# Eight products of the unit matrix between two rows of a weight product, and a later start of one unit's attention pieces

## The chip, the cores and the metric

The kernel runs on one core of a Trainium2 chip. The metric is the device time of one launch in microseconds. The core has five engines that run side by side, each through its own instructions in order: TensorE (PE in the profile; its weight loads, which overlap its matmuls, are PEld), VectorE (DVE), ScalarE (ACT), GpSimd (POOL), and SyncE (SP), which here only issues DMAs. TensorE's clock can be granted at full or at reduced speed, which the profile shows as PEclk.

## The reference

```python
def _attn_ref(q, k, v, a_re, a_im):                    # 4 batches, 8 heads, 768 steps, 48 channels
    mag = np.sqrt(a_re * a_re + a_im * a_im)
    scale = np.minimum(mag, 0.999) / (mag + 1e-06)
    a_re_n, a_im_n = (a_re * scale, a_im * scale)
    for t in range(S):
        ar, ai = (a_re_n[:, :, t, :, None], a_im_n[:, :, t, :, None])
        new_re = ar * S_re - ai * S_im
        new_im = ar * S_im + ai * S_re
        kv = np.einsum('bhd,bhe->bhde', k[:, :, t], v[:, :, t])
        S_re, S_im = (new_re + kv, new_im)
        y[:, :, t] = np.einsum('bhd,bhde->bhe', q[:, :, t], S_re)
...
def _moe_ref(x, w1, w2, w3, w_out):                    # 3072 tokens of 384, inner width 1024
    a = x @ w1
    b = x @ w2
    h = a * b @ w3
    return (h @ w_out).astype(np.float32)
```

The four weight matrices arrive as 64-bit floats; the rest is 32-bit.

## The kernel before, in words

**Units.** The work is cut into eight units: four batches, and two halves of 384 steps in each. A unit goes through three stages.

1. Gates (`gates`): elementwise work on ACT and DVE over tiles of 128 x 1152 that turns the gates, q and k into scaled and rotated forms. `gates` is a generator whose steps are named, among them `im` and `sq` (L600, L604 on DVE), `z1` (a Ln on ACT, the first use of L586 after `sq`), `n` (L614), `z2` and `a2`. It also issues loads for the next unit: the `im` part of the next gates is loaded when two products, `kc` and `qc` (L717, L719), are through, since its buffer comes free then. When a unit's gates are done, twelve DMAs move the results into tiles KL and QL (L736).
2. Pieces (`pieces`): for each of three chunks of 128 steps, two transposes on PE (`tr`, L766), each followed by a copy into tile KT on ACT (L768); a state product (`kv`, L830), followed by an addition into T on DVE (L836); scores (`sc`, L780) into two PSUM banks, followed by two masked copies into A on DVE (L783); and outputs (`y`, L813), followed by a copy into xT on ACT (L815).
3. Feed-forward (`ffn`): sixteen halves. Each is three 128-deep products of a 128-column block of w1 or w2 with xT (L852), giving m; an even half is copied to `a` by ACT (L857) and an odd one multiplied with it by DVE into `ab` (L859). After them come sums (`sum`, four So operations on DVE, L887) and seven products p (L912: p1, p2, p4, p6, p7, p5, p3) by which two token tiles are multiplied with the folded weight w3o; p1, p2 and p4 do not read So.

**Buffers.** The transposes, kv and y share two PSUM buffers in turn (`ps_v`), so that every such tile waits until the one two before it has been read: the third transpose waits for the first copy into KT. The halves and products share four (`ps_m`).

**The start.** The product of w3 and w_out (w3o) is made first, on chip, in eight rows of 128: `row_load` fetches a row of both weights, `row_work` rounds it from 64 to 32 bits on DVE and ACT (L997 to L1014; w3s and wo_s are the results, w3s in two buffers in turn, so that row f+2 is written only when PE is done with row f), and `fuse` adds, for each of eight column blocks j, one 128 x 128 by 128 x 384 product into one of eight PSUM sums (L1150). After row 7 ACT copies the sums to w3o (L1154). In the same stretch DVE and ACT work through unit 0's gates, and SP issues the loads of unit 1's gates and of the weights w1 and w2, the moves of unit 0 into KL and QL, and then fourteen loads of v into tile V (L560), which `y` needs.

**Order.** Up to row 7, a scheduler orders DVE, ACT, POOL and SP by its own model of times, PE's order is the program's. From there the order on all engines is written out by `run`, which walks a list of PE's items and puts each step of the gates (and of the weights' rounding) where a planner with a table of durations expects its inputs to be ready. `unit(u, rest, ahead)` makes the list for unit u: the first `ahead` halves of unit u-1's feed-forward, and then unit u's pieces with what is left of that feed-forward spread between them. `ahead` is AHEAD[u].

## Time and profile before

| | us |
|---|---|
| median of three runs | 552.43 (551.7 to 552.54) |
| the profiled execution, its whole time | 552.92 |
| its span | 551.1 |
| PE busy | 521.0 (95% of the span) |
| DVE busy | 372.6 |
| POOL busy | 358.0 |
| ACT busy | 275.3 |

The whole time of the profiled execution is its span and 1.8 us around it. A row of the timeline reads: start, length, engine, line, operation, output <- inputs, shape, how often; in brackets how long the engine had been idle before, and who ended that. A matmul of 32-bit operands leaves two records, a transpose one, so that a row of fuse (8 products) is 16 records and a half (3 products) is 6. A view of windows gives for each stretch its length, PE's busy time with the number of records that began in it, the mean granted clock, and the DMA engines' busy share and rate.

### The profile page before, as it was taken

What the parts mean: (1) busy time and instruction counts of PE and PEld (TensorE: products, weight loads), DVE (VectorE), ACT (ScalarE), POOL (GpSimd) and SP (SyncE); (2) the same over time, 40 slices, a digit from 0 to 9 for tenths busy, and PEclk for the clock granted to TensorE, in tenths of its full rate; (3) what the DMA queues carried; (4) which work ended last, traced back from release to release, by engine and by line L of the source; (5) the groups of instructions that cost most, each with busy time, mean ns of one, the idle gap of its engine ahead of it and who ended that gap; (6) DMA issues with size and microseconds to landing.
All of it is one profiled execution on the core that took longest, in us unless ns stands there. A gap on an engine that the chain in (4) does not pass through costs nothing.

```text
span 551.1 us, 13443 instructions
## 1 busy us (share of the span) xinstructions
PE 521.0 (95%) x5546; PEld 370.0 (67%) x5546; DVE 372.6 (68%) x553; ACT 275.3 (50%) x391; POOL 358.0 (65%) x425
## 2 busy tenths in 40 slices
PE   4689899989999999989999999999999999999995
PEld 2345575556756795669568985687569966795585
DVE  5999589775585677867977985687669751531152
ACT  5989766465543555746467426743494232111100
POOL 1000000188888788888998888988998888888100
PEclk9899899999999999989999999999999999999999
DMA  8997956966659835492889346935793173222001
GB/s 262 339 395 236 212 167 189 253 161 162 159 141 242 223 106 132 146 207 84 245 212 218 112 129 165 215 110 152 170 224 100 58 205 83 73 65 96 1 26 39
DMA packets 73510, 89.73 MB, mean 163 GB/s; under 512 B 31840, under 2 KB 63264, under 8 KB 72672
## 3 DMA queue, kind: packets, MB, share of 16 engines
q1 hardware_dynamic: 67360, 69.78, 48.2%
q0 software_dynamic: 6080, 19.01, 11.7%
q8 instruction: 45, 0.74, 0.6%
q14 instruction: 25, 0.20, 0.1%
HBM read 65.14 MB, written 4.72 MB: 127 GB/s over the span
## 4 chain that ended last, share of the span: by engine, by line
PE 67%; DVE 14%; DMA 8%; ACT 5%; issue 3%; SPq 1%; DVEq 0%; ACTq 0%
PE m L852 35%; PE p L912 14%; PE y L813 6%; PE sc L780 5%; PE o L948 3%; DMA im<-in_a_im_dram 2%; DMA QL<-q 2%; DMA raw<-in_w_dram 2%; DVE gZ L687 2%; PE kv L830 2%; PE tp L766 2%; ACT low L1002 1%; DVE So L887 1%; DMA out_dram<-ot 1%; ACT gZ L586 1%
## 5 line engine op out<-in xcount | busy, mean ns | idle before, releaser
L852 PE MATMUL m<-xT,w1s 128*128 128x384 f32 x384 | 134.5, 487 | 1.1 <-ACT xT L815 1.1
L852 PE MATMUL m<-xT,w2s 128*128 128x384 f32 x384 | 134.8, 487 | 0.0
L852 PEld LDWEIGHTS m<-xT,w1s 128*128 128x128 f32 x384 | 72.2, 190 | 48.9 <-ACT xT L815 1.7
L852 PEld LDWEIGHTS m<-xT,w2s 128*128 128x128 f32 x384 | 71.9, 190 | 47.8
L1069 POOL TENSOR_SCALAR look<-look 128x256 f32<-128x256 f32 (+1 forms) x84 | 86.7, 1032 | 7.3
L1050 POOL TENSOR_TENSOR seen<-seen,look 128x256 bf16<-128x256 bf16 (+1 forms) x84 | 80.9, 963 | 6.8
L859 DVE TENSOR_TENSOR ab<-m,a 128x384 f32<-128x384 f32 x64 | 35.2, 551 | 69.8 <-PE m L852 66.3
L857 ACT COPY a<-m 128x384 f32<-128x384 f32 x64 | 30.2, 473 | 95.1 <-PE m L852 95.1
L1034 POOL MEMSET seen<- 128x256 bf16 x1 | 0.3, 311 | 102.3 <-DVE w2s L1014 102.3
L1068 POOL TENSOR_SCALAR look<-look 128x256 f32<-128x256 f32 (+1 forms) x44 | 51.7, 1174 | 6.1 <-DMA look<-in_a_re_dram 2.8
L1066 POOL TENSOR_TENSOR look<-look 128x256 f32<-128x256 f32 (+1 forms) x72 | 48.6, 675 | 3.5 <-DMA look<-in_w_dram 1.7
L912 PE MATMUL p<-To,So 128*128 128x192 f32 x240 | 44.1, 332 | 0.0
L1045 POOL DMA_DIRECT2D look<-in_w_dram x56 | 33.1, 591 | 16.6 <-POOL seen L1050 16.6
L815 ACT COPY xT<-y 128x384 f32<-128x384 f32 x24 | 11.5, 478 | 60.2 <-PE y L813 60.2
L1071 POOL TENSOR_TENSOR look<-look 128x256 f32<-128x256 f32 (+1 forms) x44 | 38.1, 866 | 3.7
L912 PEld LDWEIGHTS p<-To,So 128*128 128x128 f32 x240 | 38.7, 190 | 2.2 <-issue 2.0
L768 ACT COPY KT<-tp 128x384 f32<-128x384 f32 x40 | 34.0, 857 | 11.9 <-PE tp L766 11.7
L813 PE MATMUL y<-A,V 128*32 128x128 f32 x768 | 39.8, 273 | 0.1
L783 DVE COPY_PREDICATED A<-mask,sc 128x512 f32<-128x512 uint8 x48 | 32.7, 733 | 6.4 <-PE sc L780 6.2
L813 PE MATMUL y<-QL,T 96*32 96x128 f32 x640 | 35.5, 272 | 0.8 <-issue 0.8
L813 PEld LDWEIGHTS y<-A,V 128*32 128x32 f32 x768 | 34.3, 110 | 2.1 <-issue 2.0
L1150 PE MATMUL f<-wo_s,w3s 128*128 128x384 f32 x96 | 35.6, 520 | 0.0
(129 smaller groups left out, 922.4 us busy)
## 6 DMA issues: line engine op xcount, KB each, us to landing
look<-in_w_dram POOLq DMA_DIRECT2D x56, 256.0 KB, 4.0
raw<-in_w_dram SPq DMA_DIRECT2D x6, 1024.0 KB, 10.7
KL<-gR SPq DMA_DIRECT2D x24, 192.5 KB, 4.6
KL<-k SPq DMA_DIRECT2D x24, 192.5 KB, 6.1
re<-in_a_re_dram SPq DMA_DIRECT2D x24, 192.0 KB, 4.4
im<-in_a_im_dram SPq DMA_DIRECT2D x24, 192.0 KB, 4.0
k<-in_k_dram SPq DMA_DIRECT2D x24, 192.0 KB, 8.1
q<-in_q_dram SPq DMA_DIRECT2D x24, 192.0 KB, 7.4
```

The source lines that it names most:

```text
L768: nc.scalar.copy(out=KT_t[u, c][:, :, :, x].rearrange("p h d f -> p f d h"), in_=tp.rearrange("p f (d h) -> p f d h", h=H))
L813: nc.tensor.matmul(out=o, lhsT=a, rhs=b, start=s0, stop=s1)
L852: nc.tensor.matmul(out=m, lhsT=w[:, j * P // WB, f, j * P % WB:j * P % WB + P], rhs=xT_t[u][:, f], start=(f == 0), stop=(f == KD - 1))
L859: nc.vector.tensor_tensor(out=ab_t[u][:, j], in0=m, in1=got[0], op=OP.mult)
L912: nc.tensor.matmul(out=m[p], lhsT=a[:, f], rhs=b[:, f], start=(f == 0), stop=(f == KH - 1))
L1045: nc.gpsimd.dma_start(out=got.bitcast(I32)[:, 0:group[2]], in_=group[1])
L1050: nc.gpsimd.tensor_tensor(out=seen[:, 0:n], in0=seen[:, 0:n], in1=x, op=OP.add)
L1066: tt(out=x, in0=x, in1=x, op=OP.mult)
L1068: ts(out=y, in0=x, scalar1=high, scalar2=None, op0=OP.is_le)
L1069: ts(out=x, in0=x, scalar1=low, scalar2=None, op0=OP.is_ge)
L1071: tt(out=x, in0=x, in1=y, op=OP.mult)
L1150: nc.tensor.matmul(out=sums[j], lhsT=w3_t[f][:, j * P:(j + 1) * P], rhs=w3_t["wo"][:, f], start=(f == 0), stop=(f == KF - 1))
```

## The change

```diff
-    AHEAD = [0, 3, 12, 12] + [8] * (NU - 4)
+    AHEAD = [0, 3, 12, 15] + [8] * (NU - 4)
...
-    sums = []
+    sums, spare = [], []
 
     def fuse(f, j):
         if not sums:
             sums.extend([sc.rearrange("p n t -> p (n t)")[:, 0:DM] for sc in Sc] +
                         [ps_v.tile([P, DM], FP, tag="v", name="f") for _ in range(2)] +
-                        [ps_m.tile([P, DM], FP, tag="mm", name="f") for _ in range(4)])
+                        [ps_m.tile([P, DM], FP, tag="mm", name="f") for _ in range(3)])
+            spare.append(ps_m.tile([P, SB * LANES * LANES], FP, tag="mm", name="f"))
+            sums.append(spare[0][:, 0:DM])
+        for _ in range(8 if (f, j) == (4, 0) else 0):
+            nc.tensor.matmul(out=spare[0][:, DM:DM + P], lhsT=ident, rhs=ident, start=False, stop=False)
         nc.tensor.matmul(out=sums[j], lhsT=w3_t[f][:, j * P:(j + 1) * P], rhs=w3_t["wo"][:, f], start=(f == 0),
                          stop=(f == KF - 1))
```

Ahead of row 4's first product PE multiplies the 128 x 128 unit matrix by itself eight times. The result goes to the last 128 columns of the eighth sum's PSUM bank, columns 384 to 511, which nothing reads. The eighth sum is now the first 384 columns of a tile that has the whole bank.

Unit 3's pieces begin when fifteen of the sixteen halves of unit 2's feed-forward are through, rather than twelve. Of unit 2's 25 feed-forward items ten rather than thirteen are left to stand between unit 3's pieces. PE's order from the thirteenth half on, before and after (tr, kv and sc with their chunk):

```
before: ab12 tr0 ab13 tr0' ab14 ab15 tr1 kv0 tr1' p1 kv1 p2 p4 sc0 p6 sc1 y0 p7 sc2 y1 y2 p5 p3
after:  ab12 ab13 ab14 ab15 tr0 tr0' p1 tr1 kv0 p2 tr1' p4 kv1 p6 sc0 p7 sc1 y0 sc2 y1 y2 p5 p3
```

The built programs differ on the other engines in three places. On DVE, all of row 7's rounding now stands ahead of the gate step `gA` (L744) that stood before its last operation, and two later steps of those gates, k and q, change places; on ACT row 7's last copy (L1002, 128 x 384) stands ahead of one gate step. In unit 3's stretch DVE does the four So before the first addition into T and swaps a few neighbours (T, gA, A, U), and ACT does `z1` before all four of the copies into KT, where it stood between the second and the third. SP and POOL issue the same DMAs and operations in the same order.

## The prediction

> **What bounds the kernel now.** I read the busy shares first (PE 95%), then the row of granted clocks, then PE's idle time in order, and last the chain of waits.

> ```profile
> PE 521.0 (95%) x5546; PEld 370.0 (67%) x5546; DVE 372.6 (68%) x553; ACT 275.3 (50%) x391; POOL 358.0 (65%) x425
> PEclk9899899999999999989999999999999999999999
> ```

> PE bounds the kernel, and three slices out of forty have a lower clock. PE's timeline around the first place that the change touches, and around the second:

> ```profile
> 35.54 2.42 PE L1150 MATMUL f<-wo_s,w3s 128*128 128x384 f32 x7
> 40.26 2.93 PE L1150 MATMUL sc<-wo_s,w3s 128*128 128x384 f32 x4 [2.30 <-DVE wo_s L1014]
> 42.98 4.34 PE L1150 MATMUL f<-wo_s,w3s 128*128 128x384 f32 x12
> 47.16 1.45 PE L1150 MATMUL sc<-wo_s,w3s 128*128 128x384 f32 x4
> ...
> 237.02 0.88 PE L830 MATMUL kv<-vr,KT 128*32 128x48 f32 x48
> 240.27 0.55 PE L766 MATMUL tp<-ident,k 128*128 128x128 f32 x3 [2.37 <-ACT KT L768]
> ```

> After each idle time the next matmuls are slow: row 4's sixteen records take 6.90 us (40.26 to 47.16), row 5's 5.16 (47.16 to 52.32). Two windows before and after each tell why:

> ```profile
> 36.72:40.13 3.41, 1.24 (x4) 1.00 1.02 413
> 40.13:43.54 3.41, 3.28 (x5) 0.51 1.00 387
> ...
> 118.63:122.04 3.41, 1.94 (x11) 1.00 1.07 241
> 238.16:241.57 3.41, 1.30 (x9) 1.00 1.11 231
> 241.57:244.98 3.41, 3.41 (x55) 0.50 1.10 248
> ```

> The chain of waits tells what a gain at the start would have to pass:

> ```profile
> 70.33 1.91 DMA V<-in_v_dram
> 72.25 1.32 PE sc L780 x57
> 75.84 1.37 DVE A L783 x2
> ...
> 114.78 3.61 DMA im<-in_a_im_dram
> 118.57 1.36 issue
> 119.92 0.56 DVE ab L859
> 120.52 0.91 PE o L948 x2
> ```

> **The products.** Eight products of two records each; a record of 384 columns takes 0.322 us at full clock (row 5: 5.16 over 16), so one of 128 columns about 0.107, and the eight 1.72 us. The nearest other row, a transpose (three in 0.33 us), gives 0.9. They run where PE waits 2.30 us for DVE's wo_s, which does not wait for them, so either length fits: the cost on the path is nothing, and should row 3 end 0.6 us later their excess would show one for one. At 1.72 us the idle time in the window falls to 0.5 to 0.6, below the 1.47 that kept the clock; at 0.9 to 1.4, just below it. Row 4 then runs in 5.16 us and ends 1.7 us earlier, at 45.4. DVE had waited for that row too:

> ```profile
> 47.36 0.69 DVE L1009 TENSOR_SCALAR w3s<-raw 128x1024 int32<-128x1024 int32 x1 [0.76 <-DMA re<-in_a_re_dram]
> ```

> The DMA named there had nothing to do with it; w3s has two buffers, and row 6's can only be written when row 4 is through (47.16). So DVE's row 6 begins 0.76 us earlier. With row 7's rounding moved ahead of a gate step (its 0.55 us) PE can go through rows 5, 6 and 7 without a stop, and begins row 7 at about 55.85 instead of 57.48: 1.6 us won there. ACT's copies out of the sums (it waited 2.62 us for the first), unit 0's transposes and kv, and unit 1's first gates hang on that and come 1.6 us earlier.

> What of it lasts? SP's queue does not move: the moves into KL and QL begin when the loads of w1 and w2 have landed (53.5), and the fourteen loads of V end with issues at 72.7 and 73.3 that land 3.5 and 3.0 us later, at 76.2 to 76.3. The first y starts at 76.14 and needs the last head some 0.65 us later, so PE itself can gain only 0.5 us there. DVE gains more. It did its masked copies of the third scores at 78.50, behind 1.15 us of waiting for PE and a heap of gate and rounding steps, all of which now lie before y; the third scores would be done at about 77.2. The buffer that SP's next load of weights waits for (issued 80.10), the V loads and weights behind it, and through them the DVE steps that end with ab at 119.92, follow that copy: 1.3 us. I take 1.3 us; the ends are 0 (the V loads keep it all) and 1.65 (all of it lasts). From 120 on PE is the chain almost everywhere, so what is won there stays.

> [...]

> **Unit 3.** Moved: four tr, two kv, three sc and three y on PE, with four copies into KT, two T, six A and three xT behind them; none of them issues a DMA, and the order on SP and POOL stays. PE's idle 2.37 us at 240.27 ends with a copy into KT, which stood in ACT's queue behind `z1` (238.23 to 239.48); `z1` waits for `sq` (until 238.12), that for `im` on DVE at 235.04, and that for the DMA im, issued at 229.28 when `qc` was done. None of these moves. What moves is what PE has to do meanwhile. Before: four halves, three tr, kv0, until 237.9. After: four halves from 228.20 (7.75 us), two tr (0.66) and p1 (1.30), until 237.9. Then tr1 waits for the first copy, which now is itself behind `z1`: 240.27 again. kv0 waits for the second copy, 0.84 us long, until 241.0: 0.35 us more idle. Behind `z1` on ACT now stand all four copies and p1's U; each waiter is on PE. The window to 241.57 has 0.9 us of work, so half clock follows as before, 1.7 us.

> From there the same set of items (to sc0 and p6) ends at 249.9 by the durations of the trace, against 249.96. DVE's four So (3.2 us) end at 241.8 with p6 at 247.3, so they stay hidden; if they were not, p6 would come up to 3.2 us later. Taken: -0.1 us. The ends: +0.9 (the wait for the second copy and one more U and copy in full) and -4.1 (idle 2.37 and 1.7 of clock both gone).

> **The sum.** -1.3 - 0.1 = -1.4 us. The profiled execution took 552.92 (span 551.1 and 1.8 around it): 551.5. It stands 0.5 above the median of 552.43, from which the same difference gives 551.0; I say 551.2, 0.2% below the median. About 0.2% (1.1 us) is what a measurement can tell from no change.

> **The rivals.**
> - *The V loads keep the gain*, or the products do not keep the clock. For: V lands 0.1 to 0.2 us after y starts. Against: DVE's backlog is what the chain names. -0.1 us: 552.3.
> - *The wait at 120.52 grows and costs the clock*: slower. PE arrives there earlier, but ab is last in a row of DVE steps behind the DMA im (114.78). If SP and DVE stay put and PE gains 0.5 us or more, the idle time of 1.47 passes 2.0, and the next window runs at half: +1.7, with 0.1 to 0.5 won elsewhere: 553.8. It decides once PE gains 0.1 to 0.6 us more than DVE. Against: the chain runs through PE's scores and DVE's copies, so DVE should gain at least as much.
> - *Unit 3's stop goes*: if im lands 0.9 us earlier, or the window's boundary splits the idle time, 1.7 to 4.1 us go as well: 549.5 down to 547.0. For: only 0.1 to 0.7 us separate the idle time in that window (2.11) from the limit. Against: the DMA's issue hangs on DVE's `qc`, which does not move.

> **How the numbers follow.** Forecast 0.48, V loads 0.21, growing wait 0.18, unit 3's stop 0.13. The range 549.0 to 553.9 holds the forecast, the V loads, the larger part of the growing wait, and the part of the last in which only the clock is won. The forecast's own range, from 1.65 won with a little luck in unit 3 to 0.8 won, is 550.2 to 551.7; about a quarter of it (above 551.3) lies within 0.2%. Faster 0.36 + 0.13 = 0.49; the same 0.12 + 0.17 = 0.29; slower 0.18 and, of the V loads' case, 0.04 with unit 3's upper end: 0.22.

> **What would show it.** Products: x16 at L1153 in the gap, row 4 in 5.2 us at clock 1.00, row 7 ready for ACT's first w3o copy near 56.7 instead of 58.33. V: a wait on V at the first y. DVE: the masked copy of 78.50 near 77.2, the load of 80.10 near 78.8, ab of 119.92 near 118.6, and an idle time there of 1.5 or less. Unit 3: an idle time near 2.3 us before its third transpose, ended by KT, another of 0.35, and half clock after. I am wrong if row 4 is still slow, if PE's wait near 120 exceeds 2 us, or if unit 3's stop is under 1.5.

## The result and the profile after

The changed kernel took 551.84 us in the median of 20 runs (546.78 to 555.88), the kernel before, run in turn with it, 552.55 (548.47 to 556.88): a ratio of 0.9976, with a 95% interval of 0.9953 to 1.0. Two later comparisons of the same pair, with 12 runs of the changed kernel each, gave 0.9993 (0.996 to 1.0025) and 0.9994 (0.9951 to 1.0036). The differences of the three means are -1.29, -0.73 and -0.49 us, with standard errors of 0.8 to 0.9; weighted together -0.9 +- 0.5. So by these means the change gains a little, 0.1 to 0.2%, close to what these runs can tell from nothing. A ratio leaves out the runs over 1.5% above the fastest of their kernel, a difference of means takes all, so that the two can disagree, most for ahead_only below, where the ratio rests on 7 of 12 runs.

The profiled execution took 548.02 (span 546.1). First the page's busy times and granted clocks, then PE's timeline at the places that the prediction spoke of (start, length, engine, line, operation, output <- inputs, count; in brackets the idle time before and who ended it):

```profile
PE 518.3 (95%) x5562; PEld 369.9 (68%) x5562; DVE 372.2 (68%) x553; ACT 275.2 (50%) x391; POOL 365.5 (67%) x425
PEclk9899899999999999999999999999999999999999
```

```profile
35.66 1.95 PE L1153 MATMUL f<-ident 128*128 128x128 f32 x16
38.13 1.56 PE L1154 MATMUL sc<-wo_s,w3s 128*128 128x384 f32 x4 [0.52 <-DVE wo_s L1014]
39.52 4.03 PE L1154 MATMUL f<-wo_s,w3s 128*128 128x384 f32 x12
...
77.55 0.30 PE L813 MATMUL y<-A,V 128*32 128x128 f32 x2 [1.87 <-issue]
...
235.73 0.55 PE L766 MATMUL tp<-ident,gR 128*128 128x128 f32 x3 [1.62 <-ACT KT L768]
236.43 0.88 PE L830 MATMUL kv<-vr,KT 128*32 128x48 f32 x48 [0.16 <-ACT KT L768]
237.24 1.57 PE L912 MATMUL p<-w3o,ab 128*128 128x192 f32 x8
```

The products stand in the gap, 16 records in 1.95 us, and leave 0.52 us of it. Row 4's sixteen records take 1.56 and 4.03 us where they took 2.93 and 4.34: from row 4 to row 5 it is 5.26 us instead of 6.90. The slice at reduced clock at 240 us is gone: after unit 3's stop a kv takes 0.88 us and eight p 1.57, their lengths at full clock. And there is a wait of 1.87 us, at 77.55 us, that names no releaser: it lies in the y of unit 0's later chunks, six us after the first y began at 71.50 without idle time.

One profile of each does not make a comparison here. In every profile the clock changes at times that lie whole numbers of 3.41 us apart, but elsewhere in each (at 241.57 us in before, at 238.56 in before_again), and single runs of one kernel spread over 10 us. For each run the time that the clock took is one minus its granted clock, times its span; that alone averages 7.4 us over 117 runs of the kernel before, and the span follows it (1.0, 0.7 and 0.9 us per us in the three sets of 35). I therefore list for every kernel the mean of that loss, and the rest of the span.

### The profile page after: what moved, and what is told of

It reads as the page before. It is cut to its first block, busy times and chain, and to the rows that moved or that the text cites. A ratio compares the mean times of both kernels' runs of the same rounds, so it can differ in the third digit from the quotient of the medians.

```text
span 546.1 us, 13473 instructions
## 1 busy us (share of the span) xinstructions
PE 518.3 (95%) x5562; PEld 369.9 (68%) x5562; DVE 372.2 (68%) x553; ACT 275.2 (50%) x391; POOL 365.5 (67%) x425
## 4 chain that ended last, share of the span: by engine, by line
PE 78%; DVE 7%; DMA 5%; ACT 4%; issue 3%; SPq 2%; DVEq 0%
PE m L852 39%; PE p L912 16%; PE y L813 7%; PE sc L780 5%; PE f L1154 3%; PE o L948 3%; PE kv L830 2%; DMA QL<-q 2%; PE tp L766 2%; DMA im<-in_a_im_dram 2%; PE sc L1154 1%; DMA q<-in_q_dram 1%; ACT gZ L586 1%; DVE gZ L687 1%; ACT low L1002 1%
## 5 line engine op out<-in xcount | busy, mean ns | idle before, releaser
L1069 POOL TENSOR_SCALAR look<-look 128x256 f32<-128x256 f32 (+1 forms) x84 | 91.9, 1094 | 7.3
L859 DVE TENSOR_TENSOR ab<-m,a 128x384 f32<-128x384 f32 x64 | 35.3, 552 | 80.1 <-PE m L852 72.5
L1050 POOL TENSOR_TENSOR seen<-seen,look 128x256 bf16<-128x256 bf16 (+1 forms) x84 | 75.2, 896 | 6.8
L1066 POOL TENSOR_TENSOR look<-look 128x256 f32<-128x256 f32 (+1 forms) x72 | 55.4, 769 | 3.6 <-DMA look<-in_w_dram 1.7
L1068 POOL TENSOR_SCALAR look<-look 128x256 f32<-128x256 f32 (+1 forms) x44 | 50.7, 1152 | 3.9 <-DMA look<-in_a_re_dram 0.7
L1071 POOL TENSOR_TENSOR look<-look 128x256 f32<-128x256 f32 (+1 forms) x44 | 40.1, 911 | 3.7
L768 ACT COPY KT<-tp 128x384 f32<-128x384 f32 x40 | 34.1, 862 | 14.3 <-PE tp L766 14.1
L783 DVE COPY_PREDICATED A<-mask,sc 128x512 f32<-128x512 uint8 x48 | 32.8, 733 | 6.0 <-PE sc L780 5.8
L780 PE MATMUL sc<-QL,KL 96*32 96x32 f32 (+3 forms) x1536 | 32.6, 235 | 2.7 <-DVE A L783 1.9
```

What stands on the lines that cost most here:

```text
L768: nc.scalar.copy(out=KT_t[u, c][:, :, :, x].rearrange("p h d f -> p f d h"), in_=tp.rearrange("p f (d h) -> p f d h", h=H))
L780: nc.tensor.matmul(out=sc[SB * g:SB * g + SB, j, s0:C], lhsT=KL[:, x * n + j, w][:, s0:s0 + SB], rhs=QL[:, x * n + j, w][:, s0:C], start=T ...
L859: nc.vector.tensor_tensor(out=ab_t[u][:, j], in0=m, in1=got[0], op=OP.mult)
L1050: nc.gpsimd.tensor_tensor(out=seen[:, 0:n], in0=seen[:, 0:n], in1=x, op=OP.add)
L1066: tt(out=x, in0=x, in1=x, op=OP.mult)
L1068: ts(out=y, in0=x, scalar1=high, scalar2=None, op0=OP.is_le)
```

## The experiments

All were timed in five rounds beside the kernel before. "Difference" is that of the means, with its standard error; "lost" and "rest" are the clock's loss and the span without it. The kernel before in the three sets of 35 runs (beside the first four rows, the next four and the last four): lost 8.1, 7.0, 7.2; rest 541.6, 541.6, 542.8.

| kernel | median, us | ratio (95%) | difference, us | lost | rest |
|---|---|---|---|---|---|
| products_only | 551.73 | 1.001 (0.9976-1.0044) | +0.1 +- 0.8 | 6.2 | 543.6 |
| ahead_only | 550.51 | 0.9931 (0.9888-0.9974) | -1.4 +- 1.2 | 7.6 | 540.8 |
| after_again | 551.31 | 0.9993 (0.996-1.0025) | -0.7 +- 0.9 | 6.6 | 542.4 |
| before_again | 549.49 | 0.9966 (0.9935-0.9997) | -1.4 +- 1.0 | 6.7 | 541.7 |
| shift_only | 552.51 | 1.0062 (1.0026-1.0098) | +2.5 +- 0.9 | 8.5 | 542.6 |
| realign | 548.02 | 0.9956 (0.9916-0.9996) | -1.3 +- 1.0 | 6.1 | 541.2 |
| shift_more | 548.4 | 0.9984 (0.9951-1.0017) | -1.4 +- 0.8 | 5.6 | 541.6 |
| im_late2 | 551.79 | 0.9988 (0.995-1.0027) | +0.4 +- 1.0 | 7.2 | 541.8 |
| realign_again | 549.71 | 0.9948 (0.9915-0.9982) | -2.7 +- 0.7 | 5.5 | 541.8 |
| realign_12 | 550.49 | 0.9995 (0.9957-1.0033) | -0.5 +- 0.9 | 6.5 | 543.1 |
| shift_only_again | 553.5 | 1.0042 (1.0001-1.0083) | +1.8 +- 0.9 | 8.3 | 543.5 |
| after_third | 552.28 | 0.9994 (0.9951-1.0036) | -0.5 +- 0.9 | 6.8 | 542.7 |

before_again is the kernel before, word for word. It came out 1.4 us lower, and its interval leaves out 1: such an interval, from 12 runs, is a little too narrow, and no single difference below 1.5 us is taken as shown here.

From the profiles, by stage. "Unit 2" is the stretch from the first half of ffn 1 to that of ffn 2, "unit 3" from there to the first half of ffn 3; "no name" are waits that name no releaser, with the number of PE records that came before; "start of unit 2" is when it began.

| kernel | row 4, us | start of unit 2 | unit 2, us: no name | unit 3, us: stop, clock |
|---|---|---|---|---|
| before | 6.90 | 146.0 | 58.97: none | 56.97: 2.37, half |
| before_again | 5.26 | 144.2 | 58.96: none | 57.04: 2.37, half |
| ahead_only | 6.96 | 147.1 | 58.96: none | 55.61: 1.58+0.15, full |
| products_only | 5.27 | 141.5 | 59.99: 0.66 at 1742 | 57.18: 2.43, full; 1.63 at the scores |
| after | 5.26 | 140.5 | 60.50: 0.57 at 1614, 0.32 at 1742 | 55.90: 1.62+0.16, full |
| after_again | 5.26 | 140.4 | 60.82: 0.62 at 1614, 0.59 at 1742 | 56.10: 2.25+0.16, full |
| after_third | 5.16 | 143.0 | 60.81: 1.48 at 1742 | 57.16: 2.23, full; 1.17 at the scores |
| shift_only | 5.26 | 141.5 | 60.53: 1.14 at 1742 | 57.32: 2.51, half |
| shift_only_again | 6.96 | 141.0 | 61.08: 1.42 at 1742 | 58.28: 3.31, half; 0.29 at the scores |
| shift_more | 5.26 | 142.2 | 58.97: none | 56.94: 1.47+0.15, half |
| realign | 5.16 | 145.7 | 58.96: none | 57.17: 2.20+0.16, half |
| realign_again | 5.27 | 144.0 | 60.34: 1.16 at 1742 | 55.58: 1.54+0.15, full; 0.54 at the scores |
| realign_12 | 5.27 | 140.7 | 60.30: 0.90 at 1870 | 57.32: 2.44, full; 0.53 and 0.92 at the scores |
| im_late2 | 5.16 | 142.8 | 60.81: 1.48 at 1742 | 57.83: none, half; 3.44 at the scores |

**Each half of the change alone**, and both whole kernels again.

```diff
# products_only: the eight products stay
-    AHEAD = [0, 3, 12, 15] + [8] * (NU - 4)
+    AHEAD = [0, 3, 12, 12] + [8] * (NU - 4)
# ahead_only: the later start stays
-        for _ in range(8 if (f, j) == (4, 0) else 0):
-            nc.tensor.matmul(out=spare[0][:, DM:DM + P], lhsT=ident, rhs=ident, start=False, stop=False)
```

> The eight products without the later start of unit 3 (AHEAD[3] stays 12). My theory: nearly all of the gain is theirs, because row 4 keeps the full clock and the start of the kernel is about 1.3 us shorter: ratio to the kernel before 0.9975 to 0.998, row 4 in 5.2 us at clock 1.00, unit 3's idle time before its fourth transpose 2.0 to 2.5 us as before. Rival (the V loads keep the gain; the later start of unit 3 makes it): ratio 0.9995 to 1.0005. Rival (the two are worth about half each): 0.9988.

> The later start of unit 3 without the products. My theory: -0.1 us, ratio 0.9995 to 1.0005; row 4 slow whenever a window of 3.4 us falls into its idle time of 2.3 us; unit 3's idle time before its third transpose 1.5 to 2.3 us, ended by a copy into KT behind z1. Rival (unit 3 makes the gain, since PE has more to do before it stops): ratio 0.9975 with an idle time under 1.5 us and no half clock after it.

> The changed kernel once more, for a second profile and the clocks of its runs. My theory: ratio 0.9975, the mean granted clock above that of the kernel before by about 0.001 (one window of 3.4 us at half clock in 550 us is 0.003, and the products take away one that falls in about two runs of three; the single stop in unit 3 stays); in the profile row 4 at clock 1.00 and a stop of 1.5 to 2.3 us in unit 3. Rival (the single profile after was a lucky start, 1.2 us early at its first matmul): ratio 1.000.

> The kernel before, as a run of its own, for the clocks of its runs and a second profile. Every theory: ratio 1.000, which shows how far two medians of the same kernel lie apart. My theory: the runs differ by some us because the windows of 3.4 us lie elsewhere in each, so that the time falls as the mean granted clock rises, and in this profile row 4, unit 3's fourth transpose or both may keep the full clock. Rival (the windows lie the same in every run, and the scatter comes from the DMAs at the start): half clock after the same idle times as in the first profile.

The products keep row 4's clock in each of the nine profiles that have them (5.16 to 5.27 us). Without them row 4 is slow in three of five; in before_again a boundary between two windows cuts the gap of 2.30 us in two, and in shift_only row 2 ran at half clock, so that row 3 ended late and hardly a gap was left (0.18 us). The products have a price too. In after_third, shift_more, realign and im_late2 row 2 also ran at half clock, and row 4 began only when the products (and in shift_more the small ones) were done, in after_third at 38.56 us though its wo_s was ready at 37.54. Alone, the products gain nothing that can be measured: less is lost to the clock, 6.2 us, but the rest grows to 543.6, the highest of all. The later start alone has the lowest rest, 540.8, and a gain of 1.4 that its error of 1.2 does not secure. So neither expectation of the two halves held: 0.9975 to 0.998 was said for products_only, no change for ahead_only.

Where the products' gain goes is seen in unit 2. PE's busy time, records, granted clock and the DMA engines' share in that stage, before and after (windows: bounds, length, then busy time and count of each engine, clock, DMA share, GB/s):

```profile
146.01:204.98 58.97, 58.95 (x683) 42.11 (x684) 43.02 (x52) 29.99 (x41) 50.32 (x60) 1.00 0.69 170
```

```profile
140.53:201.03 60.50, 59.59 (x682) 42.32 (x683) 43.41 (x52) 30.04 (x41) 51.79 (x59) 1.00 0.72 169
```

The same records (682 and the ends of the window) at the same clock, begun 5.5 us earlier, take 1.5 us longer. Compared record by record, nearly all of it comes in at two places: 0.8 us at PE's record 1614, and 0.7 at record 1742 and the few behind it. The timeline of after shows them:

```profile
185.68 0.83 PE L780 MATMUL sc<-QL,KL 96*32 96x64 f32 x34 [0.57 <-issue]
186.44 1.57 PE L912 MATMUL p<-To,ab 128*128 128x192 f32 x8
187.94 1.32 PE L780 MATMUL sc<-QL,KL 96*32 96x128 f32 x64
189.08 0.83 PE L813 MATMUL y<-A,V 128*32 128x128 f32 x22
190.23 0.60 PE L813 MATMUL y<-A,V 128*32 128x128 f32 x10 [0.32 <-issue]
```

Both waits name nobody, and both cut a row of like products in two, where no tile changes hands. From one to the other PE works through 34 + 8 + 64 + 22 = 128 records, and as each has a weight load beside it, through 256 instructions. The DMA queues of the whole run (packets, MB, share of 16 engines) have one that belongs to no line of the kernel:

```profile
q8 instruction: 45, 0.74, 0.6%
```

45 transfers of 16 KB, 0.74 MB. PE has 2 x 5562 = 11,124 recorded instructions, so one transfer for every 247. I take it for a load of PE's own program. In after such a transfer runs from 182.9 to 184.1 us and another from 187.8 to 188.8; the waits end at 185.68 and 190.23, 2.8 and 2.4 us after its beginning. In all fourteen profiles the waits at borders end 2.2 to 3.2 us after such a transfer has begun, and 1.2 to 1.8 us after it has ended (at 143.92 in before after one that began at 141.5; at 77.55 in after after one at 75.3). The transfer at 187.8 began 2.1 us after PE had passed the wait at 185.68, and it is the next wait, at 190.23, that ends after it; at record 1742 this is so in all fourteen profiles (the transfer begins 0.7 to 4.0 us after the border before it was passed, see below).

**Is it the program, or PE's early coming?** The eight products add 16 records, 32 instructions, and so shift every border of the program by that much. Four kernels vary the length of PE's program by products of one column by one column (128 multiplications each, where one of the eight has 2.1 million), and a fifth changes the planner's order in unit 3:

```diff
# shift_only, on the kernel before; PE's program 32 instructions longer, the order of every engine that of before
+        for _ in range(8 if (f, j) == (4, 0) else 0):
+            nc.tensor.matmul(out=spare[0][0:1, DM:DM + 1], lhsT=ident[:, 0:1], rhs=ident[:, 0:1], start=False, stop=False)
# shift_more, on the changed kernel: the same with 24
# realign, on the changed kernel: 56, so that the borders are again where before had them (the products one column narrower)
+        for _ in range({(1, 0): 40, (2, 0): 16}.get((f, j), 0)):
+            nc.tensor.matmul(out=spare[0][0:1, DM + P - 1:DM + P], lhsT=ident[:, 0:1], rhs=ident[:, 0:1], start=False, stop=False)
# realign_12: realign with AHEAD = [0, 3, 12, 12]
# im_late2, on the changed kernel, in gates ahead of the step "im"
+            if u == 4:
+                ready[("im", u)] = ready.get(("im", u), 0.0) + 2.0
```

> The kernel before with eight products of one column by one column between rows 3 and 4: PE has the same 32 more instructions in its program as with the eight products, and next to no work more; every engine's order is that of before. Two theories of PE's waits that name nothing the profile shows (after: 0.57 us in the second scores of unit 2 at 185.68, 0.32 at its first y at 190.23, 1.87 at the first y of the kernel). CODE: PE waits there for its own program, which comes in loads of 16 KB, one for every 256 of its instructions; the waits lie on borders of the program and move with the number of instructions. It expects unit 2's stage (first half of ffn 1 to first half of ffn 2) 59.5 to 60.8 us with waits at PE's records 1614 and 1742 as in after, instead of 58.97 with none, and no wait at unit 1's y at 144. EARLY: PE comes 3 to 5 us earlier than the transfers of unit 2 and waits for these; it expects 58.97 and no wait in unit 2, and 0.3 to 0.75 at 144 as before. Both: row 4 in 6.9 us where the clock's window falls into the gap; time 551 to 552.5, no change.

> The changed kernel with 56 more products of one column by one column (40 before row 1, 16 before row 2, where PE waits for DVE): 128 records in all are added to before, 256 instructions, so that the borders of the program's loads fall on the same pieces as in before. CODE expects unit 2's stage back at 59.0 us without waits at the scores and the first y, a wait of 0.3 to 0.75 at unit 1's last y, as in the three profiles without products, row 4 in 5.3 us, and a time some 1 us under that of the changed kernel, 550.3. EARLY expects the waits of 0.3 to 0.6 us and a stage of 60.5 us as in the changed kernel, and its time. Should the small products take more than the 3.07 us that PE waits before row 1, rows 1 and 2 are later by the excess and the gap before row 4 shrinks.

> The changed kernel with 24 more products of one column by one column before row 4 (64 records more than before in all, half a load of the program). CODE: waits that name nothing stand again at PE's records near 599, 1614 or 1742 (or whole multiples of some 127 records away), which are now other pieces, 48 records earlier in the work: not at the 31st record of unit 2's scores and not at the 23rd of its first y. EARLY: they stay at these pieces. Row 4 comes later by what 48 small records take beyond the 0.52 us that PE still waited there, a few tenths of a us up to 2; time 551 to 553.

> The changed kernel, with the planner told that unit 4's im lands 2 us later than it had reckoned: z1 is put behind unit 3's four copies into KT on ACT, and DVE's and ACT's later steps are reordered with it. Theory: PE's stop of 1.6 us before unit 3's third transpose ends with z1 ahead of the copy, so it goes: unit 3's stage 54.0 to 54.5 us instead of 55.9, and 1.5 us off the whole, 549.8. Rival: z1 later makes unit 4's gates and its moves later, and what is won is waited for in unit 4's stage (64.0 grows by 1 to 3 us): no change or slower, 551.3 to 553.

What is waited for is settled by the counts. A window from 0 to just ahead of each such wait tells how many PE records were begun: the later y of unit 0 in after (which an expectation above calls the first y of the kernel), unit 2's first y in after and in shift_only, and the cut scores of realign_again:

```profile
0.00:77.53 77.53, 61.87 (x599) 39.09 (x600) 66.71 (x143) 64.64 (x103) 2.36 (x12) 0.96 0.94 283
0.00:190.21 190.21, 172.15 (x1742) 111.47 (x1743) 145.65 (x238) 123.76 (x181) 78.88 (x104) 0.98 0.84 230
```

```profile
0.00:191.24 191.24, 172.98 (x1742) 110.80 (x1743) 146.59 (x238) 124.13 (x181) 78.41 (x104) 0.97 0.81 228
```

```profile
0.00:189.95 189.95, 171.40 (x1742) 111.04 (x1743) 144.40 (x234) 123.30 (x181) 76.89 (x102) 0.98 0.82 226
```

The same record numbers, whatever work stands there. Over all fourteen profiles such waits come at 471 to 475, 599 or 600, 727, 1233 or 1234, 1362, 1614, 1742, 1870, 2378, 2506 and 4670 records, all within a few instructions of one grid of some 127 records, which creeps by one instruction in eighty records (I take it for instructions that leave no record). The pieces move instead: where realign_again has 1742 records behind it PE stands at the 47th of unit 2's 64 scores, in after and shift_only at the 23rd of y. The only others without a name lie at unit 3's first scores, off the grid, at 2204 to 2324 records; there im_late2's profile names the transfer (below). So CODE's word on the place held: shift_only waited at 1742 (not at 1614), and shift_more at 475 and 600, on other pieces, though with no wait in unit 2 and, at 548.4 us, below the 551 to 553 that was said.

Whether PE has to wait at a border is another matter, and there EARLY has its part. Unit 2 takes 58.96 or 58.97 us in the five profiles without such a wait and 59.99 to 61.08 in the nine with one, and of these nine all began unit 2 by 144.0 us, of the five all but shift_more after that. So realign's first profile met its expectation, 58.96, but it came late, at 145.7; realign_again and realign_12 came early and waited, at other pieces. Both expectations of 59.0 for them failed. The reading that fits all: a border costs where PE comes to the next one before the load has landed, and that load shares the DMA engines with the moves and loads of unit 2 (from 187.4 to 188.2 us in after it took 7.5% of their time, two other queues 65.5 and 26.8%).

At record 1742 the traces bear this out. Without a wait PE takes 3.9 us from border 1614 to there on the changed kernel's grid (and in shift_more), and 5.1 us on the grid of before and of the realigned kernels. The transfer begins 0.7 to 4.0 us after PE has passed border 1614, and a wait, where there is one, ends 2.2 to 2.5 us after that beginning. With 3.9 us of work the seven profiles whose transfer began 2.1 to 3.4 us after the border all wait, and shift_more's, which began at 0.7, does not. With 5.1 us the five in which it began at 1.9 to 3.0 show no wait, and realign_again's, at 4.0, does. So the length of the program sets how much work lies between two borders, and the time at which the transfer begins decides the rest. That the sharing of the DMA engines makes it begin late was not tried by itself.

> The kernel of realign a second time, beside the changed kernel on one chip. CODE: unit 2's stage 59.0 us with no wait that names nothing, and a time 1 to 2 us under that of the changed kernel run beside it; about 0.3% under before. If the first result was the luck of the clock's windows: the same time as the changed kernel, within 0.5 us.

> The eight products and the 56 small ones, with unit 3's pieces twelve halves in as in before: the products alone, with the program's borders on the pieces where before has them. CODE: unit 2's stage 59.0 us; span less the time that the clock takes (one minus the granted clock, by the span) 541 to 541.8 us as in before, not the 543.6 of the products alone, and 1 us less lost to the clock: 549 to 550, 0.2% under before. EARLY: 543 and over, no faster than before.

> The kernel of shift_only a second time: only the 32 instructions more. CODE: a wait at the 23rd record of unit 2's first y (PE's record 1742) again, stage over 59.5 us, and slower than before by 0.6 to 1.5 us (0.1 to 0.3%). If the first result (0.6% slower) was chance: within 0.5 us of before.

> The changed kernel once more, for the comparison with realign: 0 to 0.8 us under before; waits at PE's records 599, 1614 and 1742; unit 2's stage 60.5 us; unit 3's stage 55.9 where its clock is kept and 57.1 where a window at half clock falls in it.

In time the length of PE's program made a difference beyond the noise. shift_only does no work that counts and leaves the order of all engines alone, and is 2.5 and 1.8 us slower, together 2.1 +- 0.6. By the table 1.4 and 1.1 us of that are the clock's loss and only 1.0 and 0.7 the rest, so that the waits at borders are not shown to be the whole of it. The way back is weaker evidence: realign is 1.3 and 2.7 us faster than before, together 2.3 +- 0.6, and 2.2 +- 0.9 faster than the changed kernel beside it in the last set, and it is the fastest of all that ran twice; but realign_12, with before's grid and the products, gained only 0.5 +- 0.9 where some 1.1 (0.2%) was expected, and its rest, 543.1, is that of before beside it, 542.8.

By which border the time goes is not settled. shift_only's two profiled executions (spans 548.7 and 548.9) are no longer than before's (551.1 and 549.9). They come to unit 3 even earlier, at 202.1 us, than the three without products on before's grid (203.1 to 206.1), in spite of the wait in unit 2. So they show the waits but not the loss.

**Unit 3's stop.** Of im_late2's profile, PE ahead of unit 3's first scores:

```profile
241.74 1.57 PE L914 MATMUL p<-To,So 128*128 128x192 f32 x8
246.75 1.32 PE L782 MATMUL sc<-QL,KL 96*32 96x128 f32 x64 [3.44 <-DMA QL<-q]
```

With z1 behind the copies into KT the stop at the third transpose is gone, as the theory said; but PE then came 3.44 us before the moves into QL had landed, unit 3 took 57.83 us, and the whole came out no faster. The time is the rival's, the place is not: the rival had unit 4's stage grow, and that took 63.85 us against 64.05 in after. Behind the stop stand the moves into QL. The same scores waited 1.63 us in products_only and 1.17 in after_third.

## Why the prediction was right or wrong

The forecast was -1.4 us, three comparisons give -0.9 +- 0.5, and 551.2 lies 0.6 below the first median. Step by step:

- **Row 4: right, but only where the window falls into the gap.** Products of 1.95 us (1.72 was said), 0.52 us left of the gap (0.5 to 0.6), row 4 in 5.26 (5.2). From row 4 to ACT's first copy into w3o it was 58.33 - 40.26 = 18.07 us before and 54.56 - 38.13 = 16.43 after: the 1.6 us. But row 4 was slow in only three of five profiles without the products, which makes the mean gain 1.0 us rather than 1.6. And in four of nine profiles with them row 3 ended late and row 4 began some 1.0 us or more after its wo_s was ready. That is the case that the prediction named ("should row 3 end 0.6 us later") and left out of its sum. The profile of before was taken as the rule for where the windows lie. The later profiles show that the place of the windows varies (a change at 241.57 us in before, at 238.56 in before_again), while the fall of the clock after a gap of 2.3 us stands as the trace had it: row 4 took 6.90 us after one of 2.30 in before, and 6.96 in ahead_only.
- **"SP's queue does not move": it held, but the profile of before was a late one.** SP's fourteen loads of V, in before, before_again (the same kernel) and after, a line from each:

```profile
63.29 10.46 SPq L560 DMA_DIRECT2D V<-in_v_dram  x14
```

```profile
58.84 9.58 SPq L560 DMA_DIRECT2D V<-in_v_dram  x14
```

```profile
58.79 10.53 SPq L560 DMA_DIRECT2D V<-in_v_dram  x14
```

The 4.5 us between the first and the last are therefore not the change's doing: the kernel before scatters by as much. In before_again the last V landed at 70.1, 2.9 us ahead of the first y at 72.98, so that the limit of 0.5 us on PE's gain, which the prediction read off the V loads at 76.2, belonged to one execution. The load of weights that the prediction followed was issued at 80.10 in before, 77.51 in before_again and 75.48 in after (78.8 was said), and unit 2 began at 146.0, 144.2 and 140.5. From one profile of each the gain at the start cannot be told to better than these 2 to 3 us.
- **The wait for ab near 120** was 1.47 us in before, none in after, 1.48 in after_again and no longer in any profile, and no window at half clock followed it; so the rival in which it grows is out.
- **V did not hold PE up.** In after the first y began at 71.50 without idle time. The 1.87 us stand in later y, and what was late there was PE's program: the wait comes at 599 records in every profile on that grid. A wait for V shows only in realign_again, 0.30 and 0.56 us, with V named.
- **"What is won there stays": the step that failed.** From 120 on PE is the chain almost everywhere, but not everywhere: in the nine profiles that wait there, 1 to 2 us go in unit 2 at borders of the program. Of the 5.5 us by which after began unit 2 earlier than before, 4.0 were left at unit 3. No row of the profile of before hinted at them except one of 0.75 us at 143.92, which named nobody and which the prediction does not mention. What a kernel adds to PE's program was costed by its time alone; shift_only shows 2.1 +- 0.6 us for 32 instructions without work.
- **Unit 3: the term of -0.1 was mis-sized.** With the later start the stage takes 55.6 to 56.1 us in four of seven profiles and 56.9 to 57.2 in three; with twelve halves 57.0 to 57.3, once 58.3. The mean gain is 1.0 us, but more than half of it does not last: over this stage and the next, to the first half of ffn 4, the means are 120.2 and 120.6 us (in after PE waits 1.11 us for A in unit 4's scores, which before did for 0.28). Where the window at half clock still follows (57.17 in realign, 56.94 in shift_more, against 56.97 and 57.04 of before's two profiles) it is about nothing, as computed; the clock was kept in five of seven, against two of six with twelve. The stop lasted 1.5 to 2.3 us, with 0.15 rather than 0.35 behind it, and lies at the limit that the prediction gave as 1.5 to 2.1; what was a rival at 0.13 is the commoner case. The limit was read from an incomplete list: the clock of before also changed at 64.07 and 70.90 us, after a window with 1.90 us of PE's work, next to the 1.94 that kept it.

That the sum came out near is in part luck. Row 4's gain was put at its full size where it comes in about three of five executions, and the loss at borders was not foreseen; against these stands unit 3, where the clock is kept more often than the prediction reckoned.

## What to carry to other kernels

An instruction can cost by its place in the program as well as by its time: here 32 more with next to no work moved the waits of PE, which runs 11,124, to other pieces, and the time rose by 2.1 +- 0.6 us. A wait that names nobody and cuts a row of like instructions in two should be checked against the queue of instruction loads and the count of instructions before it. Where the clock changes at other times in each profile, as here, read several of the kernel before, and count a gap's cost by how often it is followed by a lower clock (row 4: three of five without the products). A term that depends on a threshold near its limit belongs into the sum with its odds, not as what one profile shows.

## What the runs showed of the hardware

- The queue named instruction moved 45 transfers of 16 KB in 546 us, taken here for loads of PE's program; among scores and y PE went through 256 instructions in some 4.5 us (185.68 to 190.23 in after). Waits at their borders (0.30 us at 142.06 in before_again, 2.47 at 81.13 in ahead_only) came in all fourteen profiles, and ended 1.2 to 1.8 us after the transfer had ended.
- Unchanged work scatters: the kernel before ran from 546.39 to 558.7 us, and 12 runs of it came out 1.4 us below 35 others taken in turn with them.
- PE's busy time in a window does not alone decide the clock of the next. Unit 3's stop in shift_more (1.47 and 0.15 us) and in after_again (2.25 and 0.16), the window that it falls into and the next (PE's busy time and records, clock, DMA):

```profile
234.14:237.55 3.41, 1.78 (x54) 1.00 1.11 240
237.55:240.96 3.41, 3.41 (x13) 0.50 1.10 247
```

```profile
232.81:236.22 3.41, 1.52 (x10) 1.00 1.08 253
236.22:239.63 3.41, 2.89 (x61) 1.00 1.10 220
```

1.78 us of work were followed by half clock, 1.52 by full. In the fourteen profiles, after the first 10 us, every window at full clock with less than 1.5 us of work was followed by half clock; with 1.5 to 2.1 us both came. What else counts these runs do not show; in shift_more's window most records are kv of 48 columns, in after_again's p of 192.
